# A two-layer attention and expert kernel, from scheduled stages to steps of 32 slots in a fixed order

## The chip, the cores and the metric

The kernel runs on one core of a Trainium2 chip. The metric is the device time in microseconds (us) of one execution. The engines are named as the profile names them: PE is TensorE (PEld its weight loads), DVE is VectorE, ACT is ScalarE, POOL is GpSimd, and SP is SyncE, whose queue (SPq) issues every transfer of this kernel.

## The reference

Layer one is attention over 4 batches, 8 heads, 768 positions and head size 64, where a query sees 8 global keys and the last 96 local ones, with a distance bias. Its output, with heads side by side, is the input of layer two: four causal single-head attention experts of width 64, of which each position uses the best two.

```
scores = scale * q @ k.T + bias            # bias = -slope[h] * distance
scores = where(is_global | is_local, scores, -1e9)
x = softmax(scores) @ v                    # (4, 768, 512), heads side by side
logits = x @ w_gate                        # 4 experts; the router
w = softmax(two largest logits)
for e in range(4):
    q, k, v = x @ wq[e], x @ wk[e], x @ wv[e]
    ye = softmax(causal(scale * q @ k.T)) @ v @ wo[e]
    out += (w of e where e was chosen, else 0) * ye
```

## The kernel before

The work is cut into 24 units u, each 128 rows of one batch (six units a batch). Each unit goes through these stages.

- `prep` loads k, q and v (L177), casts them to 16 bits on POOL (L182 and L191), turns k and q on PE (L184) and copies them out on DVE (`qkT`, L188). POOL also writes a column of ones beside v (L190), which makes the row sums come out of the same matmul. For the first unit of a batch it makes the tiles of the global keys (L194 to L206, with four small loads, L197).
- `global_scores` serves three units at once (L219, L223, L228). `local_scores` runs two halves: a bias through an identity matmul (L240), pairs of matmuls on 64 rows each (L250), and an Exp on ACT (L253).
- `local_values` makes two halves of `zps` (L265, L270), each divided on DVE (L274, L276) into `x`, and turns `x` on PE (L279) and copies it (L283, `xT`).
- `project` makes the k and q of the experts (`pps`, L293; `kq`, L297) and their v and the logits (`vps`, L301, L305, L308). POOL writes ones beside that v, too (L304). On each third unit `top_two`, the router, runs for three units (L373 to L388): ten DVE instructions and one Exp on ACT, on 12 elements a row.
- `causal_scores` has one to three blocks (L326, Exp L329) and two masks on POOL (L333). `causal_values` follows (L343, L347 to L351, `zs`), then the turning of `zs` (L355, L359), the output projection (`ops`, L362), a copy on ACT (`osb`, L365) and the store (L366).

The expert weights come in four transfers through one buffer (`wst`, `bufs=1`, L134 to L148): each waits until POOL has cast the one ahead. PSUM has eight banks: `psS` two buffers of two banks for scores, `psZ` two of one for values, `psT` two of one for all the rest.

The main loop emits stages with lags (steps behind the first), and the framework's scheduler then sorts the instructions of each engine by its own priorities. Within one engine the order is fixed when the program is built, so an instruction that waits holds up all that stand behind it on that engine.

```
    L_SCORES, L_GLOBAL, L_VALUES, L_PROJECT, L_CSCORES, L_CVALUES = 1, 3, 4, 5, 6, 8
    for s in range(NU + L_CVALUES):
        for lag, stage in ((L_CVALUES, causal_values), (L_CSCORES, causal_scores),
                           (L_PROJECT, project), (L_VALUES, local_values)):
            if 0 <= s - lag < NU:
                stage(s - lag)
```

Of the kernel before, what the change touches and what calls it, by code (L numbers as in the profile page):

```python
# [17 lines left out]
HUGE = 1.0e30  # L18
# [5 lines left out]
def kernel(  # L24
# [106 lines left out]
    def load_weights():  # L131
        for src, dst in ((moe_wq, wq16), (moe_wk, wk16)):
            w32 = wst.tile([P, E, NK, Hd], F32, name="w32", tag="w32")
            dma(w32[:, :, :, :], src.rearrange("e (ko kp) d -> kp e ko d", kp=P))  # L134
            for ko in range(NK):
                G.tensor_copy(dst[:, ko, :, :, :],
                              w32[:, :, ko, :].rearrange("p (a b) d -> p a b d", b=2))
        w32 = wst.tile([P, E, NK, Hd], F32, name="w32", tag="w32")
        dma(w32[:, :, :, :], moe_wv.rearrange("e (ko kp) d -> kp e ko d", kp=P))
        for ko in range(NK):  # L140
            G.tensor_copy(wvg16[:, ko, 0:E * Hd].rearrange("p (e d) -> p e d", e=E),
                          w32[:, :, ko, :])
        wg32 = wst.tile([P, NK, E], F32, name="wg32", tag="wg32", bufs=1)
        dma(wg32[:, :, :], moe_w_gate.rearrange("(ko kp) e -> kp ko e", kp=P))
        G.tensor_copy(wvg16[:, :, E * Hd:E * Hd + E], wg32[:, :, :])
# [15 lines left out]
    NA = 4  # L161
    abuf = []
    for i in range(NA):
        a = big.tile([P, 2, NP, WP], F16, name=f"abuf{i}")
        G.memset(a[:, :, :, W:WP], 0.0)
        abuf.append(a)


    qk, vs, gl, ags, xTs, q2s, k2s, v2s, lgs, wts, a2s = ({} for _ in range(11))

    def prep(u):

        b, ri = divmod(u, NT)
        f = {}
# [4 lines left out]
        tp = psT.tile([P, 2, NP, P], F16, name="tp", tag="t")  # L179
        for i, nm in enumerate("kq"):  # L180
            s16 = pp.tile([P, H, Dh], F16, name="s16", tag="s16", bufs=4)
            G.tensor_copy(s16[:, :, :], f[nm][:, :, :])  # L182
            for p in range(NP):
                nc.tensor.transpose(tp[:, i, p, :],  # L184
                                    s16[:, 2 * p:2 * p + 2, :].rearrange("j h d -> j (h d)"),
                                    ident[:, :])
        qk[u] = pp.tile([P, 2, NP, P], F16, name="qkT", bufs=7)
        V.tensor_copy(qk[u][:, :, :, :], tp[:, :, :, :])  # L188
        vs[u] = pp.tile([P, H, VW], F16, name="v16", bufs=7)
        G.memset(vs[u][:, :, Dh:VW], 1.0)  # L190
        G.tensor_copy(vs[u][:, :, 0:Dh], f["v"][:, :, :])  # L191
        if ri == 0:
            vgf = raw.tile([P, VW], F32, name="vgf", bufs=2)
            G.memset(vgf[:, 0:Dh], 0.0)  # L194
            G.memset(vgf[:, Dh:VW], 1.0)
            for p in range(NP):
                dma(vgf[32 * p:32 * p + 2 * NG, 0:Dh], v[b, 2 * p:2 * p + 2, 0:NG, :])  # L197
# [9 lines left out]
                            vgf[:, :].unsqueeze(1).to_broadcast([P, H, VW]),  # L207
# [4 lines left out]
    def global_scores(g):  # L212

        u0 = g * NH
# [16 lines left out]
    def local_scores(u):  # L231

        ri = u % NT
        a = abuf[u % NA]
        w = W if ri else P
        for g in range(NP // 2):
            s_ps = psS.tile([P, 2, 2, 2 * P], F32, name="sps", tag="s")
            for hh in range(2):
                flat = s_ps[:, hh, :, :].rearrange("r a n -> r (a n)")
                mm(flat[:, 0:2 * w].rearrange("r (a n) -> r a n", a=2),  # L240
                   lhsT=ident[:, :], rhs=biasT[:, hh, 2 * g:2 * g + 2, 0:w],
                   start=True, stop=False, skip_group_check=True)
            for i in range(2):
                p = 2 * g + i
                for prev in range(2 if ri else 1):
                    n = NL - 1 if prev else P
                    at = i * w + prev * P
                    for hh in range(2):
                        r = slice(hh * Dh, hh * Dh + Dh)
                        mm(s_ps[:, hh, :, :].rearrange("r a n -> r (a n)")[:, at:at + n],  # L250
                           lhsT=qk[u - prev][r, 0, p, :], rhs=qk[u][r, 1, p, 0:n],
                           start=False, stop=True, skip_group_check=True)
            S_.activation(a[:, :, 2 * g:2 * g + 2, 0:w],  # L253
                          s_ps[:, :, :, :].rearrange("r h a n -> r h (a n)")[:, :, 0:2 * w]
                          .rearrange("r h (a n) -> r h a n", a=2), func=Exp, scale=sc1)
# [384 lines left out]
```

## Time and profile before

| | |
|---|---|
| median of 2 runs | 205.42 us (204.77 to 206.07) |
| the profiled execution | 204.39 us, of which the span is 202.7 us |
| PE busy | 168.2 us (83% of the span) |
| DVE, ACT, POOL busy | 117.0, 101.9, 78.5 us |
| read and written | 21.05 MB and 6.29 MB |

The span runs from the first to the last instruction of the program; 1.7 us of the profiled time lie around it. Matmuls are pipelined and the profile models their ends, so a PE that is shown busy can still lose time: the starts of consecutive matmuls tell more than their durations.

### The profile page before, as it was taken

To read this page: it belongs to the slowest core of one execution; us is meant where nothing else is said; L and a number is where in the kernel's file an instruction comes from. 1 tells how busy PE (TensorE), PEld (TensorE's weight loads), DVE (VectorE), ACT (ScalarE), POOL (GpSimd) and SP (SyncE) were. 2 spreads that over 40 slices of the span, in tenths; PEclk is the share of its full clock that TensorE was granted. 3 is DMA by queue.
4 is the path that set the end of the run, shared out by engine and by line. 5 is a ranking of instruction groups with operands and counts; after the bars stand their busy time and mean duration, and the time that the engine had idled before them with its cause. 6 is when DMAs were issued, how large, how long until landed. Compare 5 with 4: busy or idle time off the path is not lost.

```text
span 202.7 us, 6148 instructions
## 1 busy us (share of the span) xinstructions
PE 168.2 (83%) x2486; PEld 116.5 (57%) x2486; DVE 117.0 (58%) x428; ACT 101.9 (50%) x137; POOL 78.5 (39%) x217
## 2 busy tenths in 40 slices
PE   0666954888998989998999899989998999699650
PEld 0422633665775767775766677757665767477420
DVE  7411423239865767476756675786567565947630
ACT  2214230455287675455666764555667645355630
POOL 8655554426616345474335533742320111103100
PEclk9999998599999999999999999999999999999885
DMA  6988889976179686779877679796110110011122
GB/s 137 221 165 173 168 160 259 220 164 112 35 175 227 153 170 143 191 185 193 191 181 177 136 181 229 149 230 152 57 52 3 55 52 33 22 55 65 41 103 70
DMA packets 85651, 27.80 MB, mean 137 GB/s; under 512 B 82288, under 2 KB 82288, under 8 KB 85616
## 3 DMA queue, kind: packets, MB, share of 16 engines
q1 hardware_dynamic: 85616, 27.34, 61.9%
q8 instruction: 21, 0.34, 0.8%
q14 instruction: 14, 0.11, 0.2%
HBM read 21.05 MB, written 6.29 MB: 135 GB/s over the span
## 4 chain that ended last, share of the span: by engine, by line
PE 59%; DVE 15%; DMA 9%; SPq 5%; ACT 4%; POOL 3%; issue 2%; ACTq 0%; DVEq 0%; POOLq 0%
PE pps L293 11%; PE sps L240 7%; PE ops L362 6%; PE sps L250 6%; PE vps L301 4%; PE tp L184 4%; DVE qkT L188 4%; PE zps L343 4%; PE cps L326 4%; PE xps L279 4%; SPq L177 3%; PE zps L270 3%; PE ztps L355 3%; DVE zs L351 3%; DMA qf<-in_q_dram 2%; DMA w<-in_moe_wq_dram 2%
## 5 line engine op out<-in xcount | busy, mean ns | idle before, releaser
L253 ACT ACTIVATE abuf<-sps 128x892 f16<-128x892 f32 (+1 forms) x48 | 40.2, 862 | 50.3 <-PE sps L250 50.1
L329 ACT ACTIVATE a<-cps 128x1024 f16<-128x1024 f32 (+1 forms) x48 | 42.2, 915 | 15.5 <-PE cps L326 14.7
L333 POOL TENSOR_SCALAR_AFFINE_SELECT a<-a 128x256 f16<-128x256 f16 x48 | 18.4, 407 | 53.0 <-ACT a L329 52.4
L297 DVE CAST kq<-pps 128x512 f16<-128x512 f32 x24 | 16.6, 691 | 32.4 <-PE pps L293 32.4
L240 PE MATMUL sps<-biasT,ident 128*128 128x446 f16 (+1 forms) x96 | 29.3, 375 | 3.9 <-ACT a L329 1.8
L188 DVE COPY qkT<-tp 128x1024 f16<-128x1024 f16 x24 | 16.5, 688 | 23.7 <-PE tp L184 22.8
L184 PE MATMUL tp<-ident,s 128*128 128x128 f16 x192 | 18.3, 235 | 10.5 <-POOL s L182 10.3
L182 POOL CAST s<-kf 128x512 f16<-128x512 f32 x24 | 14.8, 619 | 26.0 <-issue 12.2
L365 ACT ACTIVATE osb<-ops 128x512 f32<-128x512 f32 x24 | 14.4, 598 | 17.0 <-PE ops L362 12.1
L250 PE MATMUL sps<-qkT 64*128 64x128 f16 (+1 forms) x352 | 20.4, 226 | 1.3 <-DVE qkT L188 1.3
L184 PEld LDWEIGHTS <-s 128*128 128x128 f16 x192 | 12.0, 103 | 15.5 <-POOL s L182 13.2
L276 DVE TENSOR_TENSOR x<-zps,rinv 128x256 f16<-128x256 f32 x48 | 20.2, 421 | 1.1
L270 PE MATMUL zps<-v,abuf 128*128 128x65 f16 x352 | 20.4, 194 | 0.0
L250 PEld LDWEIGHTS <-qkT 64*128 64x128 f16 x352 | 11.0, 99 | 15.4 <-issue 10.6
L270 PEld LDWEIGHTS <-abuf 128*128 128x128 f16 x352 | 18.0, 98 | 1.7 <-issue 0.4
L191 POOL CAST v<-vf 128x512 f16<-128x512 f32 x24 | 14.7, 614 | 10.8 <-DMA vf<-in_v_dram 10.7
L182 POOL CAST s<-qf 128x512 f16<-128x512 f32 x24 | 14.8, 616 | 8.3 <-DMA qf<-in_q_dram 8.3
L343 PE MATMUL zps<-v,a 128*128 128x65 f16 x336 | 16.4, 196 | 0.9 <-DVE x L276 0.9
L362 PE MATMUL ops<-wo,zt 128*128 128x512 f16 x48 | 15.3, 403 | 0.6 <-DVE n_f L590 0.3
L326 PE MATMUL cps<-kq,kq 64*128 64x128 f16 x240 | 14.8, 219 | 0.8 <-ACT a L329 0.6
L301 PE MATMUL vps<-wvg,xT 128*128 128x260 f16 x96 | 14.6, 274 | 0.8 <-DVE kq L297 0.8
L293 PE MATMUL pps<-xT,wq 128*128 128x128 f16 x192 | 15.3, 223 | 0.0
(92 smaller groups left out, 257.7 us busy)
## 6 DMA issues: line engine op xcount, KB each, us to landing
kf<-in_k_dram SPq DMA_DIRECT2D x24, 256.0 KB
qf<-in_q_dram SPq DMA_DIRECT2D x24, 256.0 KB
vf<-in_v_dram SPq DMA_DIRECT2D x24, 256.0 KB
out_dram<-osb SPq DMA_DIRECT2D x24, 256.0 KB
w<-in_moe_wq_dram SPq DMA_DIRECT2D x1, 512.0 KB
w<-in_moe_wk_dram SPq DMA_DIRECT2D x1, 512.0 KB
w<-in_moe_wv_dram SPq DMA_DIRECT2D x1, 512.0 KB
w<-in_moe_wo_dram SPq DMA_DIRECT2D x1, 512.0 KB
```

Of the source, the lines that this page charges most:

```text
L182: G.tensor_copy(s16[:, :, :], f[nm][:, :, :])
L184: nc.tensor.transpose(tp[:, i, p, :], s16[:, 2 * p:2 * p + 2, :].rearrange("j h d -> j (h d)"), ident[:, :])
L188: V.tensor_copy(qk[u][:, :, :, :], tp[:, :, :, :])
L240: mm(flat[:, 0:2 * w].rearrange("r (a n) -> r a n", a=2), lhsT=ident[:, :], rhs=biasT[:, hh, 2 * g:2 * g + 2, 0:w], start=True, stop=False ...
L250: mm(s_ps[:, hh, :, :].rearrange("r a n -> r (a n)")[:, at:at + n], lhsT=qk[u - prev][r, 0, p, :], rhs=qk[u][r, 1, p, 0:n], start=False, s ...
L253: S_.activation(a[:, :, 2 * g:2 * g + 2, 0:w], s_ps[:, :, :, :].rearrange("r h a n -> r h (a n)")[:, :, 0:2 * w] .rearrange("r h (a n) -> ...
L270: mm(z_ps[:, hq, :], lhsT=a[:, h % 2, h // 2, prev * P:(prev + 1) * P], rhs=vs[u - prev][:, h, :], start=False, stop=True, skip_group_chec ...
L293: mm(p_ps[:, i, ep, :], lhsT=w[:, ko, ep, :, :].rearrange("r a d -> r (a d)"), rhs=xT[:, ko, :], start=(i == 0 and ep == 0 and ko == 0), s ...
L326: mm(s_ps[:, e2, i, :], lhsT=k2s[b * NT + ci][r, 0, ep, :], rhs=q2s[u][r, 1, ep, :], start=(i == 0), stop=True, skip_group_check=True)
L329: S_.activation(a2[:, :, c0:c0 + len(part), :], s_ps[:, :, 0:len(part), :], func=Exp, scale=sc2)
L343: mm(z_ps[:, e, :], lhsT=a2[:, e % 2, (e // 2) * n + ci, :], rhs=v2s[b * NT + ci][:, e, :], start=(e == 0 and ci == 0), stop=True, skip_gr ...
L362: mm(o_ps[:, :], lhsT=zt[:, ep, :], rhs=wo16[:, ep, :], start=(ep == 0), stop=(ep == NEP - 1))
```

## The change

The stages are cut into smaller functions: `load`, `cast`, `turn` and `globals_in` in place of `prep`; `local_values` by halves and `turn_x`; `project_qk` by halves and `project_v`; `causal_scores` by blocks, `causal_mask`, `causal_values` by halves, `turn_z` and `output`; `weights_in` and `weights_cast`. A table of 32 slots, each a lag and a function, makes a step. Under `manual_schedule` each engine runs its instructions in the order in which the slots emit them.

On PE a step reads: k projection, (global scores), q projection, v projection, both halves of local values, causal scores 0, turning of `zs`, local scores 1, half of causal values, turning of `x`, causal scores 1, turning of k, turning of q, the other half of causal values, output, causal scores 2, local scores 0. `zs` is turned one step after it is made, and a unit's last slot has lag 9.

The other edits: `psZ` has one buffer of two banks, which both value stages use in turn. Both halves of the local values are divided by one DVE instruction. The weights come through two buffers, one transfer a step, from step 0. Columns of ones and the zeros behind the local scores are written once, the first time that a buffer of a ring is taken. The router keeps four instructions on DVE; its seven others go to POOL, spread over eight `route` slots, and its Exp no longer waits for the mask. It is computed from differences to the largest logit.

```diff
-        w32 = wst.tile([P, NEP, D], F32, name="w32", tag="w32")
-        dma(w32[:, :, :], moe_wo.rearrange("(a b) d m -> (b d) a m", b=2))
-        G.tensor_copy(wo16[:, :, :], w32[:, :, :])
...
+    def weights_in(i):
+        if i >= 4:
+            return
+        w32s[i] = wst.tile([P, E, NK, Hd], F32, name="w32", tag="w32")
+        if i < 3:
+            dma(w32s[i][:, :, :, :],
+                (moe_wk, moe_wq, moe_wv)[i].rearrange("e (ko kp) d -> kp e ko d", kp=P))
...
-    wst = fast.enter_context(tc.tile_pool(name="wst", bufs=1))
+    wst = fast.enter_context(tc.tile_pool(name="wst", bufs=2))
...
+    fast.enter_context(tc.manual_schedule())
...
-    psZ = fast.enter_context(tc.tile_pool(name="psZ", bufs=2, space=PSUM))
+    psZ = fast.enter_context(tc.tile_pool(name="psZ", bufs=1, space=PSUM))
...
+    NA, NV, NV2 = 5, 8, 2 * NT + 2
+    def ring(name, n, shape):
+        rings[name] = [big.tile(shape, F16, name=f"{name}{i}") for i in range(n)], {}
+    def take(name, u):
+        bufs, owner = rings[name]
+        first = u % len(bufs) not in owner
+        owner[u % len(bufs)] = u
+        return bufs[u % len(bufs)], first
...
+    def cast(u):
+        for nm in "kq":
+            s16s[nm, u] = pp.tile([P, H, Dh], F16, name="s16", tag="s16", bufs=4)
+            G.tensor_copy(s16s[nm, u][:, :, :], fs[u][nm][:, :, :])
+        v16, first = take("vbuf", u)
+        if first:
+            G.memset(v16[:, :, Dh:VW], 1.0)
+        G.tensor_copy(v16[:, :, 0:Dh], fs[u]["v"][:, :, :])
...
+        if hf == 0:
+            zs_[u] = psZ.tile([P, 2, 4 * P], F32, name="zps", tag="z")
...
+        if hf == 1:
+            z4 = zs_[u][:, :, 0:HG * VW].rearrange("r a (h d) -> r a h d", h=HG)
+            rinv = rinv1[:, b, ri, :].rearrange("r (a h) -> r a h", a=2)
+            V.reciprocal(rinv, z4[:, :, :, Dh])
+            x16s[u] = pp.tile([P, 2, HG, Dh], F16, name="x16")
+            V.tensor_tensor(x16s[u][:, :, :, :], z4[:, :, :, 0:Dh],
+                            rinv.unsqueeze(3).to_broadcast([P, 2, HG, Dh]), op=Alu.mult)
...
+    def route(_):
+        for g in sorted(routing):
+            if next(routing[g], "end") != "end":
+                return
...
         V.reduce_max(m1[:, :], lg[:, :, :], axis=Ax.X)
...
+        yield
+        el = tile_of("el", E)
+        G.tensor_tensor(el[:, :, :], lg[:, :, :], bc(m1), op=Alu.subtract)
+        ex = tile_of("ex", E)
+        S_.activation(ex[:, :, :], el[:, :, :], func=Exp)
+        yield
+        ge = tile_of("ge", E)
+        G.tensor_scalar(ge[:, :, :], el[:, :, :], 0.0, -HUGE, op0=Alu.is_ge, op1=Alu.mult)
+        G.tensor_tensor(ge[:, :, :], ge[:, :, :], el[:, :, :], op=Alu.add)
+        yield
+        m2 = tile_of("m2")
         V.reduce_max(m2[:, :], ge[:, :, :], axis=Ax.X)
...
+        yield
+        d = tile_of("d", E)
+        G.tensor_tensor(d[:, :, :], el[:, :, :], bc(m2), op=Alu.subtract)
+        G.tensor_scalar(d[:, :, :], d[:, :, :], 0.0, None, op0=Alu.is_ge)
+        G.tensor_tensor(ex[:, :, :], ex[:, :, :], d[:, :, :], op=Alu.mult)
+        yield
+        z = tile_of("z")
+        V.reduce_sum(z[:, :], ex[:, :, :], axis=Ax.X)
         V.reciprocal(z[:, :], z[:, :])
...
+        yield
+        G.tensor_tensor(wt[:, :, :], ex[:, :, :], bc(z), op=Alu.mult)
...
+    slots = [
+        (5, project_k),
...
+        (7, route),
+        (7, route),
+        (7, route),
+        (8, cv0),
+        (1, cast),
...
+    for s in range(min(lags), NU + max(lags)):
+        for lag, slot in slots:
             if 0 <= s - lag < NU:
```

Three places in the order of the instructions follow. The first is POOL in the middle of the program, around the casts of k, q and v of one unit (`s` and `v`). Before, with the waits that the program holds:

```order
L333 AFFINE_SELECT a_1877<-a_1877 128x2x128 [waits Activation_49]
L333 AFFINE_SELECT a_1877<-a_1877 128x2x128
L190 MEMSET v_2352 128x8 [waits PE_49]
L182 CAST s_2162<-kf 128x512 [waits DMAHW4_49,Pool_49]
L182 CAST s_2168<-qf 128x512 [waits DMAHW5_49,Pool_49]
L191 CAST v_2176<-vf 128x8x64 [waits DMAHW6_49]
```

After, in a step that has router work (one step in three; `el`, `ge`, `d` and `wt` are the router's):

```order
L481 TENSOR_TENSOR el<-lg,m_2689 128x12 [waits DVE_49]
L486 TENSOR_SCALAR ge<-el 128x12 [waits Pool_49]
L487 TENSOR_TENSOR ge<-ge,el 128x12 [waits Pool_49]
L224 CAST s_2711<-kf 128x512 [waits DMAHW6_49,PE_49]
L224 CAST s_2713<-qf 128x512 [waits DMAHW7_49,PE_49]
L228 CAST vbuf_160<-vf 128x8x64 [waits DMAHW0_49]
L422 AFFINE_SELECT a2_2344<-a2_2344 128x256 [waits Activation_49]
L422 AFFINE_SELECT a2_2344<-a2_2344 128x256
L493 TENSOR_TENSOR d<-el,m_2731 128x12 [waits DVE_49]
L494 TENSOR_SCALAR d<-d 128x12 [waits Pool_49]
L495 TENSOR_TENSOR ex<-ex,d 128x12 [waits Activation_49,Pool_49]
```

The casts now stand behind three router instructions, of which the first waits for DVE's reduction `m` of the same step.

The second place is DVE at the same point. Before:

```order
L305 CAST v_2261<-vps 128x4x64 [waits PE_49]
L308 COPY lg<-vps 128x4
L274 RECIPROCAL rinv_124<-zps 128x4 [waits PE_49]
L373 TENSOR_REDUCE m_2266<-lg 128x3 [waits DVE_49]
L276 TENSOR_TENSOR x_2301<-zps,rinv_124 128x256 [waits DVE_49]
L375 TENSOR_TENSOR ge<-lg,m_2266 128x12 [waits DVE_49]
L382 TENSOR_TENSOR el<-lg,m_2266 128x12
L376 SCALAR_TENSOR_TENSOR ge<-ge,lg 128x12 [waits DVE_49]
L379 TENSOR_REDUCE m_2271<-ge 128x3 [waits DVE_49]
L283 COPY xT<-xps 128x512 [waits PE_49]
```

After, in a step with router work:

```order
L376 CAST v2buf_166<-vps 128x4x64 [waits PE_49]
L380 COPY lg<-vps 128x4
L334 RECIPROCAL rinv_124<-zps 128x8 [waits PE_49]
L336 TENSOR_TENSOR x_2653<-zps,rinv_124 128x512 [waits DVE_49]
L456 COPY zt<-ztps 128x256 [waits PE_49]
L477 TENSOR_REDUCE m_2689<-lg 128x3
L346 COPY xT<-xps 128x512 [waits PE_49]
L490 TENSOR_REDUCE m_2731<-ge 128x3 [waits Pool_49]
L242 COPY qkT<-tp 128x1024 [waits PE_49]
L442 RECIPROCAL rinv_125<-zps_2698 128x4 [waits PE_49]
```

The two halves have become one, and between the reductions DVE now goes on with other work.

The third place is the start of SP's queue. Before:

```order
L177 DMA kf<-in_k_dram 128x8x64
L197 DMA vgf<-in_v_dram 16x1x64 x4
L134 DMA w_234<-in_moe_wq_dram 128x16x64
L144 DMA wg_252<-in_moe_w_gate_dram 128x4x4
L177 DMA qf<-in_q_dram 128x8x64
L177 DMA vf<-in_v_dram 128x8x64
L134 DMA w_240<-in_moe_wk_dram 128x16x64
```

After, from the third unit's loads on:

```order
L139 DMA w_202<-in_moe_wk_dram 128x16x64
L214 DMA kf<-in_k_dram 128x8x64
L214 DMA qf<-in_q_dram 128x8x64
L214 DMA vf<-in_v_dram 128x8x64
L139 DMA w_210<-in_moe_wq_dram 128x16x64
```

Weights and units now take turns, a whole unit between two weights, and the k weights come first.

## Rows read from the trace of the kernel before

**Rows 1.** The page: busy time, share of the span and instructions of each engine.

```profile
PE 168.2 (83%) x2486; PEld 116.5 (57%) x2486; DVE 117.0 (58%) x428; ACT 101.9 (50%) x137; POOL 78.5 (39%) x217
```

**Rows 2.** The chain that ended last (start, us, piece): two output projections, twelve units apart.

```profile
81.14 0.43 PE ops L362 x2
...
163.92 0.43 PE ops L362 x2
```

**Rows 3.** Window between them: its length, busy us (instructions) by engine, clock, DMA.

```profile
81.10:163.90 82.80, 78.73 (x1244) 55.40 (x1242) 54.99 (x197) 50.84 (x69) 32.91 (x82) 1.00 0.63 144
```

**Rows 4.** PE's timeline (start, us, instructions), merged runs of matmuls.

```profile
123.42 0.61 PE L293 MATMUL pps<-xT,wq 128*128 128x128 f16 x8
123.87 0.61 PE L301 MATMUL vps<-wvg,xT 128*128 128x260 f16 x4
124.41 0.37 PE L250 MATMUL sps<-qkT 64*128 64x128 f16 x7
...
125.27 0.55 PE L240 MATMUL sps<-biasT,ident 128*128 128x446 f16 x2
125.75 0.37 PE L250 MATMUL sps<-qkT 64*128 64x128 f16 x8
126.06 0.62 PE L184 MATMUL tp<-ident,s 128*128 128x128 f16 x8
126.52 0.89 PE L343 MATMUL zps<-v,a 128*128 128x65 f16 x24
127.34 0.23 PE L326 MATMUL cps<-kq,kq 64*128 64x128 f16 x2
...
127.52 0.22 PE L326 MATMUL cps<-kq 64*128 64x128 f16 x2
127.67 0.28 PE L265 MATMUL zps<-vg,ag 128*128 128x260 f16 x1
127.79 0.41 PE L270 MATMUL zps<-v,abuf 128*128 128x65 f16 x8
```

**Rows 5.** Waits of PE's weight loads, 81.1 to 163.9 us: us in total, times, longest.

```profile
PEld L355 <- DVE zs L351: 4.7, 11, 1.1
```

**Rows 6.** Groups by line and shape: count, busy us, mean ns, idle before.

```profile
L276 DVE TENSOR_TENSOR x<-zps,rinv 128x256 f16<-128x256 f32 x48 | 20.2, 421 | 1.1
L297 DVE CAST kq<-pps 128x512 f16<-128x512 f32 x24 | 16.6, 691 | 32.4 <-PE pps L293 32.4
...
L305 DVE CAST v<-vps 128x256 f16<-128x256 f32 x24 | 10.0, 418 | 0.7 <-PE vps L301 0.7
L274 DVE RECIPROCAL rinv<-zps 128x4 f32<-128x4 f32 x48 | 8.4, 175 | 4.5 <-PE zps L270 4.5
L308 DVE COPY lg<-vps 128x4 f32<-128x4 f32 x24 | 3.6, 151 | 0.0
...
L199 POOL TENSOR_TENSOR kg<-kmask,qkT 128x128 f16<-128x128 f16 x4 | 1.6, 404 | 0.1
L190 POOL MEMSET v<- 128x8 f16 x24 | 2.7, 138 | 3.0 <-PE zps L270 3.0
L145 POOL CAST wvg<-wg 128x16 f16<-128x16 f32 x1 | 0.2, 198 | 0.0
```

**Rows 7.** POOL's timeline at the start: the cast of the fifth unit's q.

```profile
33.71 0.61 POOL L182 CAST s<-qf 128x512 f16<-128x512 f32 x1 [0.24 <-DMA qf<-in_q_dram]
```

**Rows 8.** SP's timeline at the start: issues of transfers.

```profile
10.48 0.38 SPq L134 DMA_DIRECT2D w<-in_moe_wq_dram  x1
...
35.65 1.14 SPq L177 DMA_DIRECT2D qf<-in_q_dram  x1
```

**Rows 9.** Window at the start, columns as in group 3; the clock is the third from the right.

```profile
38.00:39.00 1.00, 1.00 (x13) 1.00 (x11) 0.00 (x0) 0.65 (x2) 0.28 (x1) 0.50 1.37 226
```

**Rows 10.** PE's timeline shortly before that, with the wait ahead of the run.

```profile
34.38 0.61 PE L184 MATMUL tp<-ident,s 128*128 128x128 f16 x4 [1.88 <-POOL s L182]
```

**Rows 11.** The chain's last output projection.

```profile
195.97 0.61 PE ops L362 x2
```

More of the change, by code (lines that the diff above doesn't have):

```diff
@@ L173, in prep, with load @@
+    fs, qk, gl, ags, xTs, kqs, lgs, wts, a2s, as_, done = ({} for _ in range(11))
+    s16s, zs_, x16s, routing, zss, zts, tps, ppss, zs2 = ({} for _ in range(9))
+    def load(u):
         b, ri = divmod(u, NT)
-        f = {}
+        f = fs[u] = {}
         for nm, src in (("k", k), ("q", q), ("v", v)):
@@ L229, in global_scores, with local_scores @@
         ags[g] = ag
-    def local_scores(u):
+    def local_scores(u, g):
         ri = u % NT
-        a = abuf[u % NA]
-        w = W if ri else P
[L236 to L255, printed above, removed]
@@ L257, in local_values @@
-    def local_values(u):
+        if u not in as_:
+            as_[u], first = take("abuf", u)
+            if first:
+                G.memset(as_[u][:, :, :, W:WP], 0.0)
+        a = held("abuf", u)
+        w = W if ri else P
+        s_ps = psS.tile([P, 2, 2, 2 * P], F32, name="sps", tag="s")
+        for hh in range(2):
+            flat = s_ps[:, hh, :, :].rearrange("r a n -> r (a n)")
+            mm(flat[:, 0:2 * w].rearrange("r (a n) -> r a n", a=2),
+               lhsT=ident[:, :], rhs=biasT[:, hh, 2 * g:2 * g + 2, 0:w],
+               start=True, stop=False, skip_group_check=True)
@@ L319, in causal_scores @@
         blocks = [(ep, ci) for ep in range(NEP) for ci in range(n)]
[L320 to L330 removed]
+        part = blocks[4 * c:4 * c + 4]
@@ new lines, in causal_scores @@
+        if not part:
+            return
+        s_ps = psS.tile([P, 2, 4, P], F32, name="cps", tag="s")
+        for i, (ep, ci) in enumerate(part):
+            for e2 in range(2):
+                r = slice(e2 * Hd, e2 * Hd + Hd)
+                mm(s_ps[:, e2, i, :], lhsT=kqs[b * NT + ci][r, 0, ep, :],
+                   rhs=kqs[u][r, 1, ep, :], start=(i == 0), stop=True,
+                   skip_group_check=True)
+        S_.activation(a2[:, :, 4 * c:4 * c + len(part), :], s_ps[:, :, 0:len(part), :],
+                      func=Exp, scale=sc2)
@@ L338, in causal_values @@
         b, ri = divmod(u, NT)
         n, a2 = ri + 1, a2s[u]
-        z_ps = psZ.tile([P, E, VW], F32, name="zps", tag="z")
-        for e in range(E):
+        assert done["m", u]
+        if i == 0:
+            zs2[u] = psZ.tile([P, 2, 4 * P], F32, name="zps2", tag="z")
+        z_ps = zs2[u][:, 0, 0:E * VW].rearrange("r (e d) -> r e d", e=E)
+        for e in range(i * E // 2, (i + 1) * E // 2):
             for ci in range(n):
                 mm(z_ps[:, e, :], lhsT=a2[:, e % 2, (e // 2) * n + ci, :],
-                   rhs=v2s[b * NT + ci][:, e, :], start=(e == 0 and ci == 0), stop=True,
+                   rhs=held("v2buf", b * NT + ci)[:, e, :], start=(e == 0 and ci == 0), stop=True,
@@ L345, in causal_values @@
                    skip_group_check=True)
+        if i == 0:
+            return
+        assert next(routing[u // NH], "end") == "end"
         rinv = rinv2[:, b, ri, :]
```

301 lines of the change are left out of this document (175 added, 126 removed).

## The prediction

> **What bounds the kernel now.** I read the page's busy line first: PE has 168.2 us of a 202.7 us span, the others far less [rows 1]. Then the chain of waits: it runs mostly through PE, and two output projections twelve units (two whole batches) apart lie 82.78 us apart, so a step takes 6.90 us [rows 2]. In that window PE is shown busy for 78.73 of 82.80 us at full clock [rows 3], which looks like a full engine. Because the profile models the ends of matmuls, I then looked at starts, to see what a step costs PE when nothing is late [rows 4]:
>
> - k and q projections: 8 matmuls from 123.42 to 123.87, so 0.45 each, 0.90.
> - v projection: from 123.87 to 124.41 is 0.54, with one change of shape (below): 0.45.
> - local scores: a bias pair from 125.27 to 125.75 (0.48) and eight 64-row matmuls to 126.06 (0.31), each with one change: 0.39 + 0.22, twice, 1.22.
> - turning k and q: 126.06 to 126.52, 0.46; turning `x`, four of the same, 0.23; turning `zs`, two, 0.11.
> - causal values: 24 in 0.82 with one change, 0.030 each; 14 on average, 0.42.
> - causal scores: pairs at 0.06 (three from 127.34 to 127.52); 7 pairs on average, 0.42.
> - local values: 0.12 to the first of eight at 0.030, two halves, 0.72.
> - output 0.43 [rows 2]. The global scores I estimate at 0.1 a unit, from four-way groups at the price of a pair.
>
> A change between matmuls on 64 rows and on 128 costs extra: the last pair before 127.67 takes 0.15 instead of 0.06, so 0.09. The sum is 5.46 us. In the new order a step changes shape eight to ten times, 0.75, so the floor is 6.2 us. Before, 6.90 - 6.2 = 0.7 us of each step is waiting. The largest named part is the turning of `zs`, which waits for DVE: 4.7 us in the window, 0.4 a step [rows 5].
>
> **The steady step.** Turning `zs` one step after it was made takes that wait away: DVE has several us in between. What comes next is whether DVE keeps up in the new order. After the q projection DVE does `kq` 0.69, `v2` 0.42, `lg` 0.15, the reciprocal 0.18 and the joined `x`; two halves now take 0.42 each, and one instruction of 512 columns out of PSUM takes 0.69 as `kq` does, so 0.69 to 0.84 [rows 6]. That is 2.13 to 2.28, and 2.35 to 2.5 with 0.2 for the last matmul to land. PE meanwhile has the v projection, local values, causal scores 0, the turning of `zs` and local scores 1: 0.45 + 0.72 + 0.24 + 0.11 + 0.61, and four changes, 2.5. So the single `psZ` buffer is free just in time; the cover is 0 to 0.15 us, and where it is gone each us of DVE's delay costs one on PE in every step. The second drain, of `zs`, has two projections of k and q and the v projection over it, 1.35 against about 1.0. The other PSUM buffers have over 1 us between a drain and the next use, and ACT has 101.9 us of work in all, so I charge nothing there. Joining the divisions saves DVE time that hides behind PE, and costs nothing.
>
> The rings remove 26 of 48 small POOL instructions (of 0.138 each for v), and with them idle POOL time ended by PE (3.0 us for L190) [rows 6]. POOL is busy for 78.5 us [rows 1], so in the steady part this is worth nothing; at the start it is inside the next term.
>
> **The new wait.** In one step of three the router's first three POOL instructions stand ahead of the casts, and the casts feed the turning of k and q in the same step. They wait for DVE's first reduction, which stands after `x` and the copy of `zt`: counted from the end of the q projection, 2.4 + 0.3 + 0.16, 2.9 us. POOL's price for 12 elements isn't in the trace; the nearest rows are 0.198 for a cast of 16 and 0.404 for a two-input instruction of 128 [rows 6]. I take 0.2, nearest in size, and 0.07 between dependent ones: 0.8, then 0.61 for k, so k is there at 4.3. PE reaches the turning of k after 2.5, half of the causal values (0.24), the turning of `x` (0.23) and causal scores 1 with two changes (0.42): 3.4. It waits 0.9, and 0.3 more for q, which comes some 0.6 after k while four turnings take 0.23: 1.2 us. Behind it are queued all of PE's later work. Six router steps still have casts (units 2, 5, up to 17 projected), so 7 us. The bounds are 0 (POOL ahead of PE) and 11 us (0.4 an instruction, 0.6 more in each). The later router parts, on POOL after the masks and on DVE after `zs`, end before `kq` of the next step can start.
>
> The Trainium skill speaks against this move: "GPSIMD Engine Reference", section "Engine selection", puts elementwise work on VectorE and calls GpSimd about twice as slow for two inputs. Here one two-input POOL row has 404 ns, for ten times the elements [rows 6], so it can't settle it; by the rule the wait would be at the long end, as in the second rival.
>
> **The start.** Before, the fifth unit's q is cast at 33.71 [rows 7], since each weight waits for the cast of the one ahead. Transfers can go faster: a 256 KB load issues in 1.14 us when the queue is full [rows 8]. Up to the fifth unit's q there are 14 loads and three weights of two loads' size: 20 x 1.14 = 22.8 us, plus about 1 before the first and 2.4 for four small loads (an estimate, half of 1.14 each), 26; it has landed and been cast at 27 to 28. I take 27. By then PE has done about 11 us of its work (five units turned, three and a half with local scores, two with local values, one projected). Of 24 x 6.2 = 148.8, 137.8 remain. From there PE is the slower side: a unit's loads take 3.4 us, one more weight 2.3.
>
> At the start PE also ran at half clock: 0.50, so 1.2 of 2.4 GHz, at 38 us, while it was full [rows 9], after a wait of 1.88 us for POOL's cast [rows 10]. Half of a 5 us stretch is 2.5 us lost; the new order has such waits too, and I keep that.
>
> **The end.** With long lags the last steps hold little work, and there the drains lie bare: in two steps the division of `x` (0.8 each, since local scores are missing above it), in three the wait for `zs` (0.6 each), and the last turning: 5 us. From the last projection at 195.97 to the end of the span there are 6.7 us before [rows 11], and nothing in that part changes.
>
> **The sum.** 27 + 137.8 + 7 + 2.5 + 5 + 6.7 = 186.0 us of span, 16.7 less than before. With 1.7 around the span the profiled time is 187.7, and since the median of the runs lies 1.0 above the profiled 204.39, the prediction is 189. It can be told from no change: 2% of 205.42 is 4 us.
>
> **Rivals.**
>
> 1. *Casts free.* POOL stays ahead in the router steps as well, since DVE's reduction comes earlier than I count. Without the 7 us: 182. For it: POOL's low load [rows 1]. Against it: the order puts the reduction behind `x`.
> 2. *Router dear.* POOL takes 0.4 or more per small instruction, and the wait in a router step is 1.8: 4 us more, 193. For it: the 404 ns row [rows 6].
> 3. *Clock.* Waiting for loads up to unit 8 keeps PE at half clock for 18 us instead of 5: 9 lost instead of 2.5, 195 to 196. For it: [rows 9]; against it: PE ran at full clock through the long window [rows 3]. The Trainium skill, "TensorE: Matmul & The Clock Gate", section "What's actually happening", says that the throttle is the default and activity releases it, which is the direction of this row.
> 4. *Order too rigid, slower.* The one `psZ` buffer serves both value stages, and DVE comes late to the reciprocal because `kq`, `v2` and `lg` stand ahead of it. If its drain lies bare (reciprocal 0.18, `x` 0.69 to 0.84, and 0.2 to land, 1.1 to 1.2 us) in each of some 21 steps, that is 25 us: 214. It is slower by over 2% from 1.0 us a step on. For it: a cover of 0 to 0.15. Against it: a late DVE loses by its lateness only, and DVE is idle for much of a step.
> 5. *Nothing moves.* The scheduler's order was as good, because it filled waits as they came, and what is won at the start is lost at the end: 205.
>
> **How the numbers follow.** The forecast has 0.50, the rivals 0.13, 0.14, 0.09, 0.08 and 0.06. A range from 180 to 200 holds the forecast (bounds of the new wait: 182 to 193), and rivals 1 to 3; it leaves out 4 and 5, 0.14, and edges. Faster by over 2% are the first four cases, 0.86; within 2% is 5 and the mild part of 4, 0.08; slower is the rest of 4, 0.06.
>
> **What would show it.** Right: output projections 6.5 to 6.7 us apart in the steady part; no wait of the turning of `zs` for DVE before the last steps; waits of about 1.2 us in all of the turning of k for POOL in each third step; the fifth unit's q cast at 27 to 28; the last output projection at about 179. Wrong: waits of causal values or of the turning of `x` for DVE's division in every step (rival 4), a clock of 0.50 after 45 us (rival 3), or router instructions of 0.4 us (rival 2). The term that I trust least is the cover over the division, because it is small and in every step.

## The result, and the profile after

The changed kernel takes 191.13 us (median of 2 runs, 190.69 to 191.58) against 205.42: a ratio of 0.930, 95% interval 0.915 to 0.946. It is faster, inside the range and 2 us over the predicted 189. The profiled execution took 190.69 us, of which the span is 188.9.

The page's busy line after, beside [rows 1]:

```profile
PE 156.4 (83%) x2486; PEld 109.0 (58%) x2486; DVE 107.5 (57%) x332; ACT 101.1 (54%) x137; POOL 86.7 (46%) x244
```

PE has the same 2486 matmuls and is shown busy for 12 us less. PE's timeline after, at two output projections twelve units apart, as in [rows 2]:

```profile
62.08 0.59 PE L463 MATMUL ops<-wo,zt 128*128 128x512 f16 x2
...
140.28 0.59 PE L463 MATMUL ops<-wo,zt 128*128 128x512 f16 x2
```

That is 78.20 us, 6.52 a step, where [rows 2] had 6.90. Within it PE is shown busy for 74.18 us, where [rows 3] has 78.73, at a clock of 1.00 and with as many matmuls: so part of its busy time before was waiting. What PE and its weight loads waited for from 45 to 150 us, all of PE's rows and the first of PEld's that names another engine (us in total, times, longest):

```profile
PE tp L235 <- POOL s L224: 4.7, 10, 1.0
PE zps L435 <- DVE x L336: 0.4, 1, 0.4
...
PEld L235 <- POOL s L224: 6.4, 10, 1.2
```

The wait for `zs` of [rows 5] is gone. In its place stands the wait that the prediction named, of the turning of k and q for POOL. PE's and POOL's timelines in a router step:

```profile
99.03 0.28 PE L407 MATMUL cps<-kq,kq 64*128 64x128 f16 x4
100.30 0.40 PE L235 MATMUL tp<-ident,s 128*128 128x128 f16 x4 [0.99 <-POOL s L224]
100.86 0.40 PE L235 MATMUL tp<-ident,s 128*128 128x128 f16 x4 [0.17 <-POOL s L224]
...
98.63 0.21 POOL L481 TENSOR_TENSOR el<-lg,m 128x12 f32<-128x12 f32 x1 [8.29 <-DVE m L477]
98.93 0.27 POOL L486 TENSOR_SCALAR ge<-el 128x12 f32<-128x12 f32 x1
99.28 0.21 POOL L487 TENSOR_TENSOR ge<-ge,el 128x12 f32<-128x12 f32 x1
99.63 0.61 POOL L224 CAST s<-kf 128x512 f16<-128x512 f32 x1
```

POOL stood idle for 8.29 us until DVE had `m`; k's cast, whose data had long been there, comes 1.0 us behind `m`. At the start, PE's and POOL's timelines:

```profile
21.85 0.51 PE L276 MATMUL gps<-qkT,kg 128*32 128x128 f16 x12 [2.66 <-POOL kg L249]
...
23.91 0.93 PE L296 MATMUL sps<-biasT,ident 128*128 128x446 f16 x2
24.78 0.56 PE L306 MATMUL sps<-qkT 64*128 64x128 f16 x8
...
25.67 1.06 PE L235 MATMUL tp<-ident,s 128*128 128x128 f16 x8
26.52 0.95 PE L296 MATMUL sps<-biasT,ident 128*128 128x446 f16 x2
...
31.58 0.61 PE L235 MATMUL tp<-ident,s 128*128 128x128 f16 x8
...
19.98 1.44 POOL L155 CAST wq<-w 128x256 f16<-128x256 f32 x4 [1.78 <-DMA w<-in_moe_wq_dram]
21.39 0.41 POOL L249 TENSOR_TENSOR kg<-kmask,qkT 128x128 f16<-128x128 f16 x1
...
29.55 0.62 POOL L224 CAST s<-qf 128x512 f16<-128x512 f32 x1 [0.35 <-DMA qf<-in_q_dram]
```

The fifth unit's q is cast at 29.55, 4.2 us earlier than in [rows 7], but PE turns it only at 31.58 and waits for nothing just then: it was itself late, after 2.66 us of waiting for `kg`, and it had worked slowly (from start to next start a bias pair takes 0.87, against 0.48 in [rows 4], and the eight turnings at 25.67 take 0.85, against 0.46 there). At the end, PE's last output projection, 8.0 us ahead of the end of the span:

```profile
180.86 0.60 PE L463 MATMUL ops<-wo,zt 128*128 128x512 f16 x2 [0.39 <-DVE zt L456]
```

### The profile page after: what moved, and what is told of

It is laid out like the page before. It is cut to its first block, busy times and chain, and to the rows that moved or that the text cites. A ratio compares the mean times of both kernels' runs of the same rounds, so it can differ in the third digit from the quotient of the medians.

```text
span 188.9 us, 6081 instructions
## 1 busy us (share of the span) xinstructions
PE 156.4 (83%) x2486; PEld 109.0 (58%) x2486; DVE 107.5 (57%) x332; ACT 101.1 (54%) x137; POOL 86.7 (46%) x244
## 4 chain that ended last, share of the span: by engine, by line
PE 58%; POOL 10%; DVE 9%; DMA 8%; SPq 5%; issue 5%; ACT 2%; POOLq 0%
PE pps L357 10%; PE sps L296 7%; PE sps L306 5%; PE tp L235 5%; PE zps L435 5%; PE cps L407 5%; PE zps L328 5%; POOL s L224 4%; PE vps L371 4%; PE ops L463 4%; SPq L214 4%; DMA w<-in_moe_wq_dram 3%; PE xps L342 2%; PE zps L323 2%; DVE x L336 2%
## 5 line engine op out<-in xcount | busy, mean ns | idle before, releaser
L410 ACT ACTIVATE a<-cps 128x1024 f16<-128x1024 f32 (+1 forms) x48 | 44.0, 917 | 37.0 <-PE cps L407 36.9
L481 POOL TENSOR_TENSOR el<-lg,m 128x12 f32<-128x12 f32 x8 | 1.7, 208 | 68.6 <-DVE m L477 68.6
L296 PE MATMUL sps<-biasT,ident 128*128 128x446 f16 (+1 forms) x96 | 26.8, 364 | 1.8 <-DVE biasT L75 1.8
L435 PE MATMUL zps<-v2buf,a 128*128 128x65 f16 x336 | 17.7, 194 | 1.7 <-DVE x L336 1.4
L306 PE MATMUL sps<-qkT 64*128 64x128 f16 (+1 forms) x352 | 18.1, 222 | 0.2 <-DVE qkT L242 0.2
L346 DVE COPY xT<-xps 128x512 f16<-128x512 f16 x24 | 10.2, 425 | 13.7 <-PE xps L342 13.7
L328 PE MATMUL zps<-vbuf,abuf 128*128 128x65 f16 x352 | 17.6, 194 | 0.0
L336 DVE TENSOR_TENSOR x<-zps,rinv 128x512 f16<-128x512 f32 x24 | 16.6, 691 | 0.8
L435 PEld LDWEIGHTS <-a 128*128 128x128 f16 x336 | 13.5, 97 | 4.2 <-issue 0.7
L228 POOL CAST vbuf<-vf 128x512 f16<-128x512 f32 x24 | 14.8, 617 | 1.3 <-DMA vf<-in_v_dram 1.3
```

Of the source, the lines that this page charges most:

```text
L296: mm(flat[:, 0:2 * w].rearrange("r (a n) -> r a n", a=2), lhsT=ident[:, :], rhs=biasT[:, hh, 2 * g:2 * g + 2, 0:w], start=True, stop=False ...
L328: mm(z_ps[:, hq, :], lhsT=a[:, h % 2, h // 2, prev * P:(prev + 1) * P], rhs=held("vbuf", u - prev)[:, h, :], start=False, stop=True, skip_ ...
L336: V.tensor_tensor(x16s[u][:, :, :, :], z4[:, :, :, 0:Dh], rinv.unsqueeze(3).to_broadcast([P, 2, HG, Dh]), op=Alu.mult)
L410: S_.activation(a2[:, :, 4 * c:4 * c + len(part), :], s_ps[:, :, 0:len(part), :], func=Exp, scale=sc2)
L435: mm(z_ps[:, e, :], lhsT=a2[:, e % 2, (e // 2) * n + ci, :], rhs=held("v2buf", b * NT + ci)[:, e, :], start=(e == 0 and ci == 0), stop=Tru ...
```

## The experiments

Each kernel is timed against the kernel before, and differs from the kernel after by the edit shown, where nothing else is said.

### The router's place on POOL

```diff
-        (7, route),
-        (7, route),
-        (7, route),
         (8, cv0),
         (1, cast),
+        (7, route),
+        (7, route),
+        (7, route),
```

> One thing is changed against the kernel after: the three route slots that stand ahead of the casts are put behind them, so that POOL casts k, q and v before it waits for DVE's reduction. Theory 1 (the new wait of each third step is this queueing and nothing else): the turning of k and q no longer waits for POOL in the steady part (10 waits with 6.4 us in the trace of after, 1.4 us in each router step), and 6 to 9 us go: 182 to 185 us. Rival: the router's chain itself is late, and the wait turns up elsewhere (the masks that causal values need, or DVE's second reduction): less than 3 us gained, 188 to 191 us.

Measured: 182.88 us (ratio 0.893, interval 0.887 to 0.899), 8.2 less than after. PE has one wait left from 45 to 150 us, the whole answer:

```profile
PE zps L435 <- DVE x L336: 0.2, 1, 0.2
```

In each of the six router steps with casts the distance from one k projection to the next is shorter than in the kernel after, by 1.15, 1.21, 1.06, 1.39, 1.07 and 1.20 us: 7.1 us. The rest is at the start. Theory 1 holds and the rival falls: the wait moved nowhere.

The second kernel leaves the slots alone and runs the seven instructions on DVE (`G.tensor_...` to `V.tensor_...` in `top_two`).

> One thing is changed against the kernel after: the router's seven instructions that went to POOL run on DVE, in the same places of the order; slots and formulas are the same. Theory 1 (what costs is that POOL's casts stand behind a wait for DVE): the waits of the turnings for POOL go, 8 us; DVE has seven more instructions of about 0.2 us in each third step, of which those ahead of the copy of xT and of qkT hide behind PE: 183 to 185 us. Rival (DVE is needed on time there: the three ahead of xT and the three ahead of qkT, 0.6 each, come out as waits of PE, 0.6 to 1.2 us in each of 8 router steps): 188 to 193 us.

Measured: 185.42 us (0.904, 0.898 to 0.911). Here too the waits for POOL are gone, so what cost 7 us was casts behind a wait for DVE. The lines of PE's waits:

```profile
PE cps L407 <- DVE kq L362: 0.9, 2, 0.5
PE zps L435 <- DVE x L336: 0.8, 3, 0.3
PE pps L357 <- DVE qkT L242: 0.5, 2, 0.3
```

DVE is now late at three places, and the kernel is 2.5 us slower than with the casts first; the intervals just meet. Part of that lies in the instructions themselves, in the groups by line of this kernel:

```profile
L494 DVE TENSOR_SCALAR d<-d 128x12 f32<-128x12 f32 x8 | 3.8, 478 | 0.3
L501 DVE TENSOR_TENSOR wt<-ex,z 128x12 f32<-128x12 f32 x8 | 3.4, 423 | 0.3
...
L481 DVE TENSOR_TENSOR el<-lg,m 128x12 f32<-128x12 f32 x8 | 1.4, 171 | 0.3
```

Twelve elements cost DVE 171 to 478 ns, and cost POOL 208 to 269 (the rows above show `el` and `ge`). So the router on POOL was right, by 2.5 us; its place ahead of the casts was wrong, by 8.2.

### The turning of zs, and the fixed order

```diff
-        (9, turn_z),
         (2, ls1),
...
         (8, cv1),
+        (8, turn_z),
         (9, output),
```

> One thing is changed against the kernel after: zs is turned right behind the causal values that make it, in the same step and not one step later (the output follows at once). Theory 1 (the delay by a step is what removed PE's wait for zs): PE waits for the last matmul to land, the reciprocal, ce and zs, about 1.0 us a step, and then for the copy of zt ahead of the output, about 0.5 more: 24 to 36 us slower than after, 207 to 225 us, more than the kernel before. Rival: the wait was small in the kernel before (4.7 us in twelve steps, 0.4 a step) because the scheduler placed other work in it, and in a fixed order it's about as small: 8 to 12 us, 199 to 203 us.

Measured: 231.71 us (1.124, 1.115 to 1.134), 40.6 over after and beyond theory 1's bound. PEld's longest waits from 45 to 150 us:

```profile
PEld L452 <- DVE zs L446: 18.2, 12, 2.1
```

The windows of the same stretch and of one microsecond behind such a wait (columns as in group 3 of before; the clock is the third number from the right):

```profile
45.00:150.00 105.00, 84.28 (x1232) 58.21 (x1230) 51.43 (x150) 49.28 (x68) 40.29 (x110) 0.90 0.60 128
...
103.00:104.00 1.00, 1.00 (x13) 0.91 (x10) 0.00 (x0) 0.78 (x2) 0.00 (x0) 0.50 0.00 0
```

And PE's timeline there, where the eight matmuls of a k projection take 0.83 to the next start:

```profile
101.78 0.29 PE L452 MATMUL ztps<-ident,zs 128*128 128x128 f16 x2 [1.99 <-DVE zs L446]
...
103.09 1.03 PE L357 MATMUL pps<-xT,wk 128*128 128x128 f16 x8
103.92 1.06 PE L357 MATMUL pps<-xT,wq 128*128 128x128 f16 x8
```

The edit does one thing less than its expectation says: the output keeps lag 9, so it stays a step behind, and the 0.5 us charged for the copy of `zt` does not arise; PE waits for no `zt` in this stretch. The wait for `zs` is 1.5 us a step, not 1.0, since the 0.69 us copy of `qkT` stands ahead of the reciprocal on DVE. The theory had no second loss: the granted clock is 0.50 from 103 to 105 us, the 1.2 GHz level, after a wait of 1.99 us, and averages 0.90 in the stretch; I estimate 0.10 x 105, about 10 us, for its twelve steps. The two make 2.3 us a step, and a step is 2.2 us longer than after. The rival falls: what the scheduler hides for 0.4 a step lies bare in a fixed order.

Without `manual_schedule` the same slots are sorted by the scheduler:

```diff
-    fast.enter_context(tc.manual_schedule())
```

> One line is changed against the kernel after: the fixed order is switched off, so the framework's scheduler sorts the same slots' instructions by its own priorities. Theory 1 (the fixed order itself carries part of the gain: a step that begins with work whose inputs are a step old): waits of PE for zs and x come back and the time goes half way or more back to before, 198 to 206 us. Rival (the smaller functions, the lags and the buffers carry it, and any order of them does): 185 to 194 us; below 189 if the scheduler moves the casts ahead of the router's instructions on POOL.

Measured: 188.4 us (0.922, 0.917 to 0.926), 2.7 under after by the medians and within its interval; its four runs spread from 186.24 to 189.59. The rival holds: the fixed order, as it was first written, earns nothing; the smaller functions, lags and buffers, between which no run tells, carry the gain. The turning's wait for POOL in that kernel, from 45 to 150 us:

```profile
PE tp L234 <- POOL s L223: 0.2, 1, 0.2
```

The scheduler put the casts ahead of the router by itself, so its router steps take 6.8 to 7.3 us from output to output and not 7.8 to 8.0; it gives some back at the start, where the first output comes at 55.9 instead of 54.3. The fixed order with the casts first does no better in between: from the first output projection to the last it takes 120.6 us (52.33 to 172.95), and so does the scheduler's (55.90 to 176.51). Its whole lead in these two traces, 3.6 us, lies ahead of the first output.

### The cover over the division, and the changes of shape

```diff
+            V.tensor_copy(pad16[:, :], pad32[:, :])
             V.reciprocal(rinv, z4[:, :, :, Dh])
```

> One independent DVE copy of 128x512 out of SBUF into SBUF (f32 to f16) is added ahead of the reciprocal of the local values in every step; nothing else. It makes the division of x late by its own length, taken as 0.3 to 0.4 us. Theory 1 (the prediction's cover over the division, 0 to 0.15 us, is right): PE loses 0.2 to 0.4 us in every one of 24 steps, as waits of causal values for x: 5 to 9 us slower than after, 196 to 200 us. Rival (the cover is larger than the added work, because causal values come late on PE for other reasons): within 1.5 us of after, 190 to 193 us.

Measured: 195.96 us (0.954, 0.947 to 0.961), 4.8 over after, 0.20 a step, just under theory 1's 5 to 9. DVE's timeline:

```profile
94.33 0.42 DVE L338 CAST pad<-pad 128x512 f16<-128x512 f32 x1
94.66 0.20 DVE L339 RECIPROCAL rinv<-zps 128x8 f32<-128x8 f32 x1
```

The copy holds up the reciprocal by 0.33, so 0.13 was covered: within the predicted 0 to 0.15. That is a mean: in the two profiled executions a step grows by 0.03 to 0.71 us, 0.28 on average, which would leave a cover of 0.05. What PE lost, from 45 to 150 us:

```profile
PE zps L440 <- DVE x L341: 4.1, 9, 0.8
```

The next kernel starts from the casts first, and joins two runs of 64-row matmuls:

```diff
-        (5, cs0),
         (2, ls1),
+        (5, cs0),
...
-        (5, cs1),
         (1, turn_q),
+        (5, cs1),
```

> Against the kernel with the casts first (e1_casts_first, 182.9 us), two pieces of PE's order are moved: causal scores 0 stand right behind local scores 1, so that two runs of 64-row matmuls become one and PE changes shape twice less in each step; and causal scores 1 stand behind the turning of k and q, to give ACT time for its Exps. Theory 1 (a change of shape costs 0.09 us, a term of the floor of 6.2 us a step): 24 x 0.18, 4.3 us less, 178 to 179.5 us. Rival 1 (the change costs nothing, the starts were later for another reason): within 1 us, 182 to 184 us. Rival 2 (causal scores 1 now wait for ACT's Exp of the local scores to give their buffer back): 0.2 to 0.4 us a step more, 187 us or above.

Measured: 184.27 us (0.901, 0.898 to 0.905), not faster than 182.88: theory 1 falls, and the time, near rival 1's, has another reason than rival 1. The two new waits from 45 to 150 us, PE's and PEld's:

```profile
PE sps L296 <- ACT a L410: 2.1, 6, 0.5
...
PEld L435 <- DVE x L336: 3.1, 14, 0.3
```

What PE saved, it waits for again: for `x`, and, at local scores 0 (not at causal scores 1), for ACT. So this move alone couldn't price the change of shape. Two kernels, both with the casts first, try to free that cover; the first moves the copy of `v2buf` from DVE to ACT and splits the bias off the local scores, the second only moves the copy.

```diff
+        (5, causal_open),
+        (2, lb1),
+        (5, cs0),
         (2, ls1),
...
-        V.tensor_copy(v2[:, :, 0:Hd],
-                      v_ps[:, 0:E * Hd].rearrange("r (e d) -> r e d", e=E))
+        S_.activation(v2[:, :, 0:Hd],
+                      v_ps[:, 0:E * Hd].rearrange("r (e d) -> r e d", e=E), func=Copy)
```

> Against e1_casts_first (182.9 us): causal scores 0 stand between the bias matmuls and the 64-row matmuls of local scores 1, so that PE changes shape twice less in each step and ACT still gets the causal scores first; and ACT, idle at that time, copies the experts' v out of PSUM (v2buf) in place of DVE, which comes 0.4 us earlier to the division. Theory 1 (in e9_fewer_shapes the 0.18 us of a step that the shapes gave back was lost again to waits for x and for ACT, since the cover over the division is about nothing): with x earlier it shows, 24 x 0.18 = 4.3 us less, 178 to 180 us. Rival (the change of shape costs less than 0.09 us, or PE waits for ACT now): 182 to 184 us.

> Against e1_casts_first (182.9 us) only the copy of the experts' v out of PSUM is moved from DVE to ACT; PE's order is that of e1_casts_first. Theory 1 (in that order PE waits for nothing in the steady part, DVE just comes in time): nothing gained but 0.5 us or so in the last steps, 181.8 to 183.2 us. Rival (part of the steady 6.12 us a step is hidden waiting for x, which the profile shows as busy): 1.5 us or more gained, under 181.5 us.

Measured: 186.52 us (0.909, 0.903 to 0.915), above both readings, and 183.91 us (0.897, 0.891 to 0.903), nothing gained: with the casts first PE waits for no `x` that a freer DVE would bring sooner, as theory 1 of the second has it. PE's timeline with a change of shape behind causal scores 0 (casts first), and without (the first of the two):

```profile
92.96 0.40 PE L407 MATMUL cps<-kq,kq 64*128 64x128 f16 x8
93.29 0.28 PE L452 MATMUL ztps<-ident,zs 128*128 128x128 f16 x2
```

```profile
88.93 0.40 PE L417 MATMUL cps<-kq,kq 64*128 64x128 f16 x8
89.16 0.36 PE L313 MATMUL sps<-qkT 64*128 64x128 f16 x8
```

The first kernel's waits from 45 to 150 us, PE's and PEld's:

```profile
PE cps L417 <- ACT a L420: 3.2, 10, 0.4
...
PEld L445 <- DVE x L343: 2.7, 14, 0.3
```

The same four pairs take 0.33 with a change behind them and 0.23 without: the predicted 0.09 is there. But causal scores 1 now wait 0.39 for ACT to give a buffer back. And a wait for `x` is there although DVE has less ahead of it: it is the last matmul's landing, the reciprocal and the product, 1.1 us in a row, and the PE work that is left above it takes 1.1 us as well. DVE's queue was not the limit there.

### The ends, and the rings

On POOL, `globals_in` goes ahead of `weights_cast`, both right behind `causal_mask`.

> One thing is changed against the kernel after: on POOL the tiles of the global keys are made ahead of the weight casts, both right behind the masks. Theory 1 (at the start PE waits 2.66 us for kg because POOL stands in the cast of the q weights, which waits for its transfer): that wait goes, the first k projection comes 2 to 3 us earlier than 27.89 and the time is 2 to 3.4 us under after: 187.5 to 189 us. Rival (the loads set the start, so that what is won at 21 us is waited for at 30): within 1 us of after, 190 to 192 us.

Measured: 191.47 us (0.937, 0.934 to 0.941), the rival's value. `kg` is no longer waited for, the first k projection comes at 25.34 and not 27.89, and then, in PE's timeline:

```profile
28.54 0.85 PE L371 MATMUL vps<-wvg,xT 128*128 128x260 f16 x4 [2.13 <-POOL wvg L161]
```

The window behind it:

```profile
28.50:32.00 3.50, 3.46 (x34) 2.15 (x35) 1.39 (x4) 0.60 (x1) 1.99 (x6) 0.54 1.10 276
```

Of the 2.55 us, 2.13 went into a wait for the next weight, and the stretch at a clock of 0.54 behind it took the rest and more: the second k projection starts at 33.73, later than the 32.80 of after.

The rings, undone: the three `if first:` are removed, so each buffer's constant columns are written every time.

> One thing is changed against the kernel after: the columns of ones beside v and beside the experts' v, and the zeros behind the local scores, are written each time that a buffer is taken, not only the first time (some 50 small POOL instructions more, about 0.14 us each). Theory 1 (they lie on an idle part of POOL, except for those ahead of the casts in router steps and at the start): 0 to 1.5 us over after, 191 to 192.5 us. Rival (each waits until PE has read the buffer's last content, and holds up the casts behind it): 4 us or more over after, 195 us and above.

Measured: 190.44 us (0.929, 0.927 to 0.932), no cost that shows. POOL is busy for 92.5 us instead of 86.7, off the path. The rings are worth nothing here.

The end: from the last output projection to the end of the span it is 8.0 us after (180.86 to 188.9) and 6.7 in [rows 11]. The next kernel (the one with the split bias, with one more edit) counts the range check of `rinv1` and `rinv2` before the last steps.

> e10_shapes_v_on_act, and besides the range check of the row sums is counted ahead of the last steps (the first layer's after step 28, the second's ahead of the last output), so that only the count's sum is left behind the last output. Theory 1 (the 1.3 us by which the end is longer than before is this check, which stands behind the last output): the span from the last output projection to the end is 6.6 to 6.9 us in place of 8.0, and the time 1 to 1.4 us under e10. Rival (the end is set by the store of the last output, not by the check): no difference, 8.0 us.

Measured: 187.37 us (0.915, 0.908 to 0.921), and 177.13 to 185.0, 7.9 us. Theory 1 falls: counting was not the cause. The last kernel (casts first) tries both ends:

```diff
-        (0, weights_in),
+        (-1, weights_in),
...
+        (-1, load_globals),
...
+        (3, globals_in),
+        (1, weights_cast),
...
+        if last:
+            last.append(nc.values_load(last[0][0:1, 0:1], min_val=0, max_val=total))
         dma(out[b, ri * P:(ri + 1) * P, :], o_sb[:, :])
```

> e1_casts_first (182.9 us) with an edit at each end. Start: each weight is transferred and cast one step earlier, the four small loads of the global values stand behind the second unit's loads, and POOL makes the tiles of the global keys ahead of the weight casts. Theory 1 (in e5_globals_first the 2.55 us that came free were given back to a wait of 2.13 us for the transfer of the expert v weights and a stretch at a clock of 0.50 behind it): with that transfer earlier, the second output projection (52.3 to 58.9 us in e1) comes 2 to 4 us earlier. Rival (the start is bound by the bytes that have to arrive): less than 1 us earlier. End: the range check is counted before the last output, and SP loads its sum ahead of the last store. Theory 1 (the 1.3 us by which the end is longer than before are the check's way through SP's queue, where the load and the branch stand behind the last store, not the counting, which e12_end_early moved without gain): the last output projection to the end of the span takes 6.7 to 7.0 us in place of 8.0. Rival (the stores set it): 7.8 to 8.0. Together, theory 1: 177.5 to 180 us; rivals: 182 to 183 us.

Measured: 186.5 us (0.909, 0.905 to 0.912). The end behaves as theory 1 says: 177.24 to 184.2, 7.0 us. The start falls: the second output projection comes at 63.20 where the casts first have 58.94. What SP's queue waited for in the first 20 us of this kernel:

```profile
SPq L140 <- DVE biasT L75: 5.8, 1, 5.8
```

Its timeline:

```profile
1.92 0.90 SPq L215 DMA_DIRECT2D vf<-in_v_dram  x1
8.69 0.37 SPq L140 DMA_DIRECT2D w<-in_moe_wk_dram  x1
9.10 1.31 SPq L215 DMA_DIRECT2D kf<-in_k_dram  x1
```

The first weight waits until DVE has made `biasT`, at 8.6 us, which fits the code, where the setup's pool is given back ahead of the weights' pool. The kernel after sent that weight at 8.67 as well, so nothing was won, and the second unit's loads, sent from 5.75 there, now stand behind it. Whether that start gains without this wait was not tried, nor the new end by itself with the casts first; I estimate from these rows that the latter gives 182.88 - 1.0, about 182.

The fastest kernel run is the one with the casts first: 182.88 us.

## Why the prediction was right

The forecast's mechanisms came true: the wait for `zs` went, the wait for POOL came, and nothing else bound the steady part. Its terms, in us of the span:

| step of the sum | predicted | measured | from |
|---|---|---|---|
| fifth unit turned | 27 | 31.6 | PE's timeline |
| router wait | 7 | 7.1 | steps after, less those with the casts first |
| PE's remaining work, half clock and bare drains | 137.8 + 2.5 + 5 | 142.2 | last output 180.9, less the two above |
| behind the last projection | 6.7 | 8.0 | PE's timeline, span |
| span | 186.0 | 188.9 | |

That the sum came within 2.9 us is partly luck: 4.6 and 1.3 too little stand against 3.1 too much. And the median lies 0.4 over the profiled time, not the 1.0 that was added, which hides another 0.6. Of the 13.8 us of span that were won, about 2.6 were won up to the turning of the fifth unit's q (34.38 in [rows 10], 31.8 after) and 12.5 from there to the last output projection; the end took 1.3 back.

- **The floor.** With the casts first, where PE waits for next to nothing in the steady part, twelve steps take 73.47 us (58.94 to 132.41), 6.12 each against the 6.2 added up from [rows 4].
- **The router.** 1.2 us a step was right to 0.02, in part by luck. POOL's three small instructions were sized well: 208 to 269 ns each, and 0.80 us from the first to k's cast in five of the six steps (1.00 in the one shown), against 0.8. But DVE's reduction was ready 2.4 to 2.6 us behind the q projection and not 2.9, so k was cast at 3.9 to 4.1 and not 4.3; and PE could turn k at 3.0 to 3.4 (read with the casts first) and not at 3.4. The two misses nearly cancel. Rival 2's 0.4 did not come. The Trainium skill, "GPSIMD Engine Reference", section "Engine selection", gives about twice DVE's time for two inputs; at this size the runs show 208 (`el` on POOL) against 171 (on DVE), and against 342 to 423 where DVE met POOL's work. What the skill's rule speaks against was right here; what cost time was the order.
- **Rival 1** became true through the experiment instead: casts free, predicted 182, measured 182.88.
- **The cover** of 0 to 0.15 measured 0.05 to 0.13 on average, and the prediction's worst case (rival 4) stayed away for the reason given: only lateness beyond it counts.
- **The start** was mis-sized by 4.6 us. The step that failed is that by 27 "PE has done about 11 us of its work": the fifth unit's q was there only 1.5 to 2.5 us later than computed (cast at 29.55), but POOL's queue had the tiles of the global keys behind a weight cast, and PE worked at half pace until 27.9. Which of the two cost more is open; without the wait for `kg` alone (globals ahead) the time stayed. The 2.5 us for the half clock were charged behind the start, where it didn't come (1.00 from 28.35 us, the first record, to 185.37): without them the third row reads 142.8 against 142.2.
- **"Nothing in that part changes"** at the end was wrong by 1.3: the sum of the check is loaded on SP (and the branch taken) behind the last store, where the scheduler had put it between two stores. The last kernel shows 1.0 of it.

## What to carry to other kernels

An instruction that waits for another engine blocks everything behind it in its own queue, so in a fixed order place the work whose inputs are long there (casts, loads) ahead of it: here one move of three slots was worth 8 us, more than half as much as the whole rewrite. When a wait is taken away, ask what is late next before counting the gain: earlier globals waited for a weight, fewer changes of shape waited for `x`, and an earlier weight held up the loads behind it. A wait on TensorE can cost more than its length, because the clock can fall behind it (0.50 behind a wait of 1.99 us, 0.54 behind one of 2.13). And where a fixed order is in question, run the same pieces under the scheduler too: here it found the better place of the casts by itself.

## What the runs showed of the hardware

A DVE instruction with two inputs in SBUF that begins while POOL works on SBUF waits for POOL. `ce`, 4 elements a row, takes 0.16 us alone and up to 0.64 beside a cast of POOL, with the casts first (DVE, DVE, POOL):

```profile
96.50 0.16 DVE L444 TENSOR_TENSOR ce<-rinv,wt 128x4 f32<-128x4 f32 x1
...
102.59 0.61 DVE L444 TENSOR_TENSOR ce<-rinv,wt 128x4 f32<-128x4 f32 x1
...
102.58 0.61 POOL L224 CAST s<-kf 128x512 f16<-128x512 f32 x1
```

Both end at 103.2; each `ce` of this kernel that took over 0.18 us ends 0.01 to 0.02 us behind a POOL instruction. The Trainium skill, "SBUF — State Buffer", section "SBUF: two separate sides", says so: a DVE instruction with two SBUF inputs contends with a GpSimd instruction that reads SBUF, and the one that comes second is blocked until the other is done. The trace agrees, and it explains the 423 ns of `wt` on DVE. `d` has one input and waits as well: in the six router steps with casts it begins under a cast and takes 0.54 to 0.65 us, in the two without 0.17. The rule for two inputs doesn't explain that; whether another of the page's conditions does is open.

Four loads of 4 KB held SP's queue for 2.81 us at the start of the kernel after, where the three of 256 KB ahead of them took 0.47 to 0.92 each; why is open:

```profile
0.80 0.47 SPq L214 DMA_DIRECT2D kf<-in_k_dram  x1
...
1.94 0.92 SPq L214 DMA_DIRECT2D vf<-in_v_dram  x1
2.90 2.81 SPq L219 DMA_DIRECT2D vgbuf<-in_v_dram  x4
```

And a clock of 1.00 in a window at the start does not mean full speed. The trace of the kernel after holds no record of the clock before 28.35 us, and a window counts time without a record as 1.00. There the bias pair took 0.87 us and not 0.48, and the eight turnings 0.85 and not 0.46, while a q projection takes 0.45 from 28.55 on. The kernel before quickens at its first record too, at 23.57: from one start to the next, four local-value matmuls took 0.24 us at 21.26, and eight took 0.24 at 23.60. The pace ahead of the first record is that of the stretch with a recorded clock of 0.50 (there the eight matmuls of a k projection took 0.83, above), so I take it for the 1.2 GHz level, though no record says so.
